# Attention steps in a fused attention and SwiGLU kernel: value products in a step of their own, PSUM banks dealt out anew

## The chip, the core and the metric

The kernel runs on one core of one Trainium2 chip. Its engines work side by side, each through its own queue in program order: TensorE (PE in the profile, its weight loads PEld), VectorE (DVE), ScalarE (ACT), GpSimd (POOL) and SyncE (SP), which here issues all DMAs. Matrix products are written to PSUM, which has eight banks of 128 partitions by 512 float32 values; DVE and ACT read them from there. The metric is the device time of one execution in microseconds (us). The kernel before took 1760.38 us, the median of three runs from 1759.78 to 1762.22.

## The reference, cut to what matters

The output is a gated mix of two branches of the same input x (2048 rows, 576 columns).

```
g = sigmoid(sum(x * gate_w))                 # one value a row
out = g * A(x) + (1 - g) * B(x)
B:  (silu(x @ w_gate) * (x @ w_up)) @ w_down          # inner width 4608
A:  32 heads of 18 columns, 4 segments of 512 rows; within a segment
    p = softmax(q @ k.T * scale + mask);  a_dot = p @ v
    a_mem = (phi(q) @ M) / (phi(q) @ z + 1e-6)        # memory of earlier segments
    o = sig(beta) * a_mem + (1 - sig(beta)) * a_dot;  then o @ wo
```

Computation is float32 in effect: operands are split into a high and a low part (`split`: ACT copies the high part, DVE subtracts it to get the low one), and three products are added.

## The kernel before, in words

There are three stages. The first (to about 212 us) makes q, k, v, the memory terms and stores them to DRAM. The second, the main loop, runs to about 1650 us and holds the change. The last mixes the branches and applies `wo`.

**The main loop** goes twice (two halves of the rows, 0 and 1) over 36 slices f of the inner width: 72 positions. A position makes seven products (`seven`, lines 973 to 981, seven matmuls of 512 columns each, numbered 0 to 6 here; a Strassen-like scheme for gate and up) in banks 0, 1 and 2. Between them ACT and DVE copy and combine the sums: line 1035 (ACT copies product 0 out of bank 0; product 2 then adds into that bank, so it has to wait for the copy), 1038, 1042, 1045, 1049, then two Silu calls at lines 1052 and 1054. Silu and Exp are in different tables of ACT, so line 1052 begins with a table load and `exp_table` (line 971) with another.

**Beats.** After each product but one `tick()` is called, eight times in a position (beats 0 to 7; beats 5 and 6 stand together after product 5). A beat first runs the small work that was deferred to it (`due`: weight splits, lines 231 to 252; hidden splits, lines 117, 118, 920, 921; stores), then down groups, then steps of attention.

**Down groups.** After every third slice the 16 down groups of these three slices come due (`feed`), and the next position, a down position, runs them: two in each of beats 2 and 3, three in each of beats 4 to 7 (`SHARE`). There are 11 such positions in each half; what is left runs at the halves' ends. A group is nine matmuls of 320 or 256 columns into one bank (line 837), then one DVE addition of that bank into `ya` (line 842). Groups take banks 3 and 4 in turn (`pair_tile`), so a group waits for the addition of the group two before it.

**Attention** is the generator `att_gen`, advanced step by step. A unit is two heads of a segment, 64 units in all. A unit has five score banks, numbered z; each is filled by one or two matmul calls (`s_bank`, line 713) and reduced by DVE to a bound a row (line 719). One step later ACT takes the exponential out of the bank into `pe` (`e_bank`, line 731) and POOL masks the diagonal (line 739); three steps after the scores (`PL`) DVE casts it to `p` and POOL subtracts for the low part (`p_bank`, lines 745, 746); five steps after (`XL`) SP issues a DMA transpose to `pt` (`x_bank`, line 750). Eight steps after the scores (`VL`), in the step of the last bank, `v_unit` multiplies the unit's five `pt` tiles with the values (40 short matmuls, lines 761, 762) and DVE reduces the sum (line 768). `o_step` scales, and a DMA stores the result.

So a unit takes five steps, and the score and value banks are taken in turn from 5, 6 and 7 (`ts_tile`), six takings a unit. There are three buffers of `pe`, four of `p`, eight of `pt`.

How fast the generator goes is set by `credit` in `beat`: each allowed slot adds a number from `TICK`, and a step runs when the sum reaches 1. Down positions have a slot after the first and the third group of a beat and one in beats 0 and 1; other positions have one in each of beats 0 to 4.

```
TICK = ((0.48, 0.85), (0.39, 0.85))      # (half 0, half 1), (no groups due, groups due)
```

When the generator ends, `c_open` loads what the last stage needs.

Of the kernel before, what the change touches and what calls it, by code (L numbers as in the profile page):

```python
# [12 lines left out]
F32 = mybir.dt.float32  # L13
F32R = mybir.dt.float32r
BF = mybir.dt.bfloat16
F16 = mybir.dt.float16
# [4 lines left out]
P = 128  # L21
# [4 lines left out]
L = 512  # L26
NSEG = 4
# [9 lines left out]
NB = 8 * NSEG  # L37
NST = 2
PL = 3
XL = 5  # L40
VL = 8
KEPT = 2
HALF = ((2, 3), (0, 1))
TICK = ((0.48, 0.85), (0.39, 0.85))
QUIET = (5, 6, 7)
LEAD = 3
HIGH = (2, 3, 3, 7, 7, 8, 9)
# [19 lines left out]
def gated_mix(ctx, tc, xT, xrest, wf, wfr, wfh, wd, wv, wo, beta, cmask, ident, bmask, out):  # L67
# [32 lines left out]
    def banks(*ids):  # L100
        turn = cycle(ids)
        return lambda shape=(P, L): ps.tile(list(shape), F32, name=f"bank{next(turn)}")
# [3 lines left out]
    pair_tile = banks(3, 4)  # L106
# [4 lines left out]
    a_tile = banks(0)  # L111
    x_tile = banks(1)
    y_tile = banks(2)
    ts_tile = banks(5, 6, 7)

    def split(hi, lo, src):
        nc.scalar.activation(hi, src, AF.Copy)
# [57 lines left out]
    VP, accs, cur, mbs = {}, {}, {}, []  # L175

    def stack_loads(u):
        s, b = divmod(u, 16)
        r = []
        for kind, t, terms in ((0, qst, (0, 0, 1)), (1, kst, (2, 1, 2))):  # L180
            d = stk[kind, s, 2 * b * DH:2 * b * DH + 2 * DH]
            r.append((t[u % NST][0:3 * DH], d.rearrange("(j r) z n -> (r z) j n", r=DH)))
            for n, z in enumerate(terms):
                r.append((t[u % NST][(3 + n) * DH:(4 + n) * DH], d[:, z].rearrange("(j r) n -> r j n", r=DH)))
        return r
# [7 lines left out]
    def v_fetch(k):  # L193
        VP[k] = ap.tile([P, 4, 8, 3, E], BF, name="v")
        nc.sync.dma_start(VP[k], vd[k // 4, k // 2 % 2][:, :, 8 * (k % 2):8 * (k % 2) + 8])
# [481 lines left out]
    with ExitStack() as st:  # L677
        cps = []
# [24 lines left out]
        ap = pool(ast, "ap", 2, side="right")  # L703
        SPLAN = [[(0, 0, 3)], [(0, 1, 3)], [(384, 0, 0), (0, 0, 2)], [(384, 1, 0), (0, 1, 2)], [(0, 0, 1), (256, 1, 1)]]

        def s_bank(z):
            u, n = divmod(z, 5)
            qs, ks = qst[u % NST], kst[u % NST]
            m = mbs[u % 2]
            t = ts_tile()  # L710
            for c, pr, i in SPLAN[n]:
                w = P * (i + 1)
                nc.tensor.matmul(t[:, c:c + w], qs[:KR, pr, P * i:P * i + P], ks[:KR, pr, 0:w],  # L713
                                 start=True, stop=True)
            for c, pr, i in SPLAN[n]:
                w = P * (i + 1)
                k = pr * 4 + i
                scr = kp.tile([P, L], BF, name="scr", bufs=1)
                nc.vector.tensor_tensor_reduce(scr[:, :w], t[:, c:c + w], cm[:, L - w:L], -SCALE, 3.0e38,  # L719
                                               OP.add, OP.min, m[:, k:k + 1])  # L720
            cur["t", z] = t

        def e_bank(z):
            u, n = divmod(z, 5)
            m = mbs[u % 2]
            t = cur.pop(("t", z))
            pe = ap.tile([P, L], F32, name="pe", bufs=3)
            for c, pr, i in SPLAN[n]:
                w = P * (i + 1)
                k = pr * 4 + i  # L730
                nc.scalar.activation(pe[:, c:c + w], t[:, c:c + w], AF.Exp, bias=m[:, k:k + 1], scale=SCALE)  # L731
            first, step = ((384, 0), (384, 0), (256, 128), (256, 128), (128, 256))[n]
            if step:
                d = bass.AP(tensor=pe.tensor, offset=pe.offset + first, ap=[pe.ap[0], [step, 2], [1, P]])
                pat = [[0, 2], [-1, P]]
            else:
                d = pe[:, first:first + P]
                pat = [[-1, P]]
            nc.gpsimd.affine_select(d, d, pattern=pat, compare_op=OP.is_ge, fill=0.0, base=0, channel_multiplier=1)  # L739
            cur["e", z] = pe  # L740

        def p_bank(z):
            pe = cur.pop(("e", z))
            p = cur["p", z] = ap.tile([P, 2, L], F16, name="p", bufs=4)
            nc.vector.tensor_copy(p[:, 0], pe)  # L745
            nc.gpsimd.tensor_sub(p[:, 1], pe, p[:, 0])  # L746

        def x_bank(z):
            pt = cur["x", z] = ap.tile([P, 8, P], F16, name="pt", bufs=8)
            nc.sync.dma_start_transpose(pt, cur.pop(("p", z)).rearrange("p a n -> p (a n)"))  # L750

        def v_unit(u):
            g, hf = divmod(u, 2)
            s, b = divmod(u, 16)
            t = ts_tile([P, 2, 4, 3 * E])
            todo = [(5 * u + n, pr, i, j, c // P + j) for n in range(5) for c, pr, i in SPLAN[n] for j in range(i + 1)]
            for n, (z, pr, i, j, c) in enumerate(todo):
                h = 2 * b + pr
                v = VP[4 * s + h // 8][:, j, h % 8].rearrange("p t e -> p (t e)")
                pt = cur["x", z]  # L760
                nc.tensor.matmul(t[:, pr, i, :], pt[:, c], v, start=(n == 0), stop=False, skip_group_check=True)  # L761
                nc.tensor.matmul(t[:, pr, i, 0:2 * E], pt[:, 4 + c], v[:, 0:2 * E], start=False,  # L762
                                 stop=(n == len(todo) - 1), skip_group_check=True)
            for n in range(5):
                cur.pop(("x", 5 * u + n))
            if hf == 0:
                accs[g] = ap.tile([P, 2, 8, E], F32, name="acc")
            nc.vector.tensor_reduce(accs[g][:, hf], t.rearrange("p a i (t e) -> p (a i) e t", t=3),
                                    axis=AX.X, op=OP.add)

        sends = []

        def o_step(g):
            s, b = divmod(g, 8)
            rz = ap.tile([P, 4, 4], F32, name="rz", bufs=1)
            av = accs.pop(g).rearrange("p r (a i) e -> p (r a) i e", i=4)
            nc.vector.reciprocal(rz, av[:, :, :, DH])
            nc.gpsimd.tensor_mul(rz, rz, omg[:, 4 * b:4 * b + 4])
            ob = ap.tile([P, 4, 4 * DH], F32, name="ob", bufs=1)
            ov = ob.rearrange("p i (h e) -> p h i e", e=DH)  # L780
            nc.gpsimd.tensor_mul(ov, av[:, :, :, 0:DH], rz[:, :, :, None].to_broadcast([P, 4, 4, DH]))
            d = atd[4 * s:4 * s + 4, :, 4 * b * DH:4 * (b + 1) * DH]
            sends.append((d.rearrange("i p n -> p i n"), ob))

        def att_gen():
            N = 10 * NB
            for tau in range(N + VL + 5):
                u, n = divmod(tau, 5)
                if tau % 10 == 4 and sends:
                    nc.sync.dma_start(*sends.pop(0))  # L790
                if n in (2, 3) and u + 1 < 2 * NB:
                    for d in stack_loads(u + 1)[4 * (n - 2):4 * n - 4]:
                        nc.sync.dma_start(*d)
                z = tau - VL
                if z % 20 == 0 and 0 <= z < N and z // 20 + 1 < 4 * NSEG:
                    v_fetch(z // 20 + 1)
                if 0 <= z - 3 and (z - 3) % 10 == 9:
                    o_step((z - 3) // 10)
                if 0 <= tau - PL < N:
                    p_bank(tau - PL)  # L800
                if 0 <= tau - 1 < N:
                    e_bank(tau - 1)
                if z % 5 == 4 and 0 <= z < N:
                    v_unit(z // 5)
                if tau < N:
                    s_bank(tau)
                if 0 <= tau - XL < N:
                    x_bank(tau - XL)
                yield
            for z in sends:  # L810
                nc.sync.dma_start(*z)
# [15 lines left out]
        def down_group(c, i, hf, hs, ws, ya, half):  # L827
            b, k = divmod(i, 4)
            cs = (slice(0, 320), slice(320, D))[hf]
            t = pair_tile([P, 320])[:, :cs.stop - cs.start]  # L830
            n = 0
            for f in range(CH * c, CH * c + CH):
                hh, hl = (z[:, b, P * k:P * k + P] for z in hs[half, f])
                d = ws[half, f]
                dh, dl = d[:, 0], d[:, 1]
                for p, q in ((hh, dh), (hh, dl), (hl, dh)):
                    nc.tensor.matmul(t, p, q[:, cs], start=(n == 0), stop=(n == 3 * CH - 1))  # L837
                    n += 1
            if c == 0:
                nc.vector.tensor_copy(ya[:, i, cs], t)  # L840
            else:
                nc.vector.tensor_add(ya[:, i, cs], t, ya[:, i, cs])  # L842
            if c == FT // CH - 1 and hf and half == 0:
                stores.append((ffd[i], ya[:, i]))
# [248 lines left out]
        for n in range(17):  # L1093
# [6 lines left out]
            if n:  # L1100
                tt = order[n - 1]
                ff = ffs.pop(n - 1)
                for hf in range(2):
                    c = slice(288 * hf, 288 * hf + 288)
                    t = chain_tile()
# [67 lines left out]
```

## Time and profile before

| what | value |
|---|---|
| median of three runs | 1760.38 us (1759.78 to 1762.22) |
| the profiled execution's own time | 1760.2 us |
| its span, first to last instruction | 1758.5 us |
| PE, PEld busy | 1720.8, 1482.1 us |
| DVE, ACT, POOL busy | 1362.9, 1096.9, 937.6 us |
| granted clock of TensorE, mean | 0.997 |

The profile is of one execution. Matmuls are pipelined and their ends are modelled: a 512-column matmul is drawn 0.39 us long while its successor starts 0.23 us after it. So PE's busy time hides short waits, and a wait shows on PE with about 0.16 us missing; the weight loads (PEld) show the same wait from their side.

### The profile page before, as it was taken

The numbers are of one execution on the slowest core, as the hardware profiler recorded it, in microseconds if no ns is written. First come the engines' busy times: TensorE is split into PE (matmuls) and PEld (weight loads), VectorE is DVE, ScalarE is ACT, GpSimd is POOL, SyncE is SP. The second block draws the span as 40 slices with busy tenths as digits, with TensorE's granted clock in tenths as the row PEclk, the third lists the DMA queues.
The fourth block names the chain that finished last, engine by engine and source line by source line (L and its number), as shares of the span: only waits on it lengthen the run. The fifth ranks groups of instructions, "written<-read, shape, count | busy, mean of one in ns | idle before, by whom it ended". The sixth has DMA issues, their size and how long they took to land.

```text
span 1758.5 us, 35163 instructions
## 1 busy us (share of the span) xinstructions
PE 1720.8 (98%) x11868; PEld 1482.1 (84%) x11868; DVE 1362.9 (78%) x3239; ACT 1096.9 (62%) x2201; POOL 937.6 (53%) x1194
## 2 busy tenths in 40 slices
PE   9999999999999999999998999999999999999999
PEld 7898978888878878878887888888888888888899
DVE  6666578888898888878888777887887778876655
ACT  7665575775676577567656657665765577566511
POOL 4434646666565666656556555555555555553221
PEclk9999999999999999999999999999999999999999
DMA  8653488998987888798779977776777778665544
GB/s 286 231 178 130 159 284 181 215 226 180 222 211 179 208 195 205 159 221 195 172 186 240 288 156 165 184 167 157 164 187 163 133 180 192 152 134 140 164 133 140
DMA packets 524005, 328.08 MB, mean 187 GB/s; under 512 B 411184, under 2 KB 460336, under 8 KB 523824
## 3 DMA queue, kind: packets, MB, share of 16 engines
q1 hardware_dynamic: 523824, 325.83, 74.3%
q8 instruction: 93, 1.52, 0.4%
q14 instruction: 88, 0.72, 0.1%
HBM read 165.76 MB, written 76.09 MB: 138 GB/s over the span
## 4 chain that ended last, share of the span: by engine, by line
PE 66%; ACT 11%; DVE 11%; issue 4%; DMA 3%; POOL 3%; SPq 1%; POOLq 0%; DVEq 0%; ACTq 0%
PE bank L978 23%; PE bank L837 22%; PE bank L140 9%; PE bank L981 4%; PE bank L713 3%; PE bank L761 2%; DVE hl L921 2%; ACT L971 2%; DVE scr L719 2%; ACT L1052 2%; DVE p L745 1%; PE bank L762 1%; ACT pe L731 1%; DMA pt<-p 1%; POOL p L746 1%
## 5 line engine op out<-in xcount | busy, mean ns | idle before, releaser
L746 POOL TENSOR_TENSOR p<-pe,p 128x512 f16<-128x512 f32 x320 | 377.4, 1179 | 479.2 <-DVE p L745 455.5
L837 PE MATMUL bank<-dw,hh 128*128 128x320 f32 (+1 forms) x2304 | 490.8, 306 | 15.2 <-DVE ya L842 8.4
L837 PEld LDWEIGHTS bank<-dw,hh 128*128 128x128 f32 x2304 | 378.2, 189 | 38.9 <-DVE ya L842 19.7
L731 ACT ACTIVATE pe<-bank,mb 128x512 f32<-128x512 f32 (+3 forms) x512 | 247.2, 523 | 249.1 <-POOL p L746 189.6
L837 PE MATMUL bank<-dw,hl 128*128 128x320 f32 (+1 forms) x1152 | 340.4, 296 | 0.3 <-DVE hl L118 0.3
L719 DVE CUSTOM_DVE_ANT_0 scr<-bank,cm 128x512 bf16<-128x512 f32 (+3 forms) x512 | 248.1, 485 | 7.5 <-PE bank L713 0.8
L842 DVE TENSOR_TENSOR ya<-bank,ya 128x320 f32<-128x320 f32 x352 | 158.1, 453 | 88.1 <-PE bank L837 87.3
L837 PEld LDWEIGHTS bank<-dw,hl 128*128 128x128 f32 x1152 | 217.8, 189 | 0.6 <-DVE hl L118 0.6
L981 PE MATMUL bank<-xr,rh 128*128 128x512 f32 x504 | 196.7, 390 | 0.0
L739 POOL TENSOR_SCALAR_AFFINE_SELECT pe<-pe 128x256 f32<-128x256 f32 (+1 forms) x320 | 147.8, 462 | 12.6 <-ACT pe L731 9.4
L745 DVE CAST p<-pe 128x512 f16<-128x512 f32 x320 | 142.7, 446 | 6.5 <-DMA pt<-p 6.5
L245 POOL TENSOR_TENSOR ws<-raw 128x256 f32<-128x256 f32 x140 | 120.3, 860 | 24.6 <-DVE wo__22862 L252 4.1
L713 PE MATMUL bank<-kst,qst 108*128 108x512 bf16 (+3 forms) x512 | 124.8, 305 | 0.0
L921 DVE TENSOR_TENSOR hl<-row,hh 128x512 fp32r<-128x512 f32 x120 | 111.1, 926 | 10.6 <-ACT hh L920 10.4
L981 PEld LDWEIGHTS bank<-xr,rh 128*128 128x128 f32 x504 | 94.9, 188 | 20.4
L1045 ACT ACTIVATE row<-bank 128x512 f32<-128x512 f32 x72 | 43.1, 599 | 87.9 <-PE bank L981 87.9
L1050 DVE TENSOR_TENSOR row<-bank,row 128x512 f32<-128x512 f32 x72 | 49.6, 689 | 58.5 <-ACT bank L1049 58.0
L1049 ACT ACTIVATE bank<-bank 128x512 f32<-128x512 f32 x72 | 41.9, 582 | 82.6 <-PE bank L981 82.2
L1052 ACT ACT_TABLE_LOAD x72 | 92.4, 1283 | 1.3
L971 ACT ACT_TABLE_LOAD x72 | 92.4, 1283 | 1.0
L140 PE MATMUL bank<-xo,qhi 128*128 128x512 f32 x264 | 83.1, 396 | 0.0
L355 POOL TENSOR_TENSOR q<-qr,q 128x512 bf16<-128x512 f32 x36 | 44.4, 1234 | 70.5 <-ACT q L354 61.4
(2165 smaller groups left out, 4130.4 us busy)
## 6 DMA issues: line engine op xcount, KB each, us to landing
raw<-in_wf_dram SPq DMA_DIRECT2D x140, 256.0 KB
rh<-rc SPq DMA_DIRECT2D x72, 336.0 KB
dc<-dw SPq DMA_DIRECT2D x36, 576.0 KB
dw<-dc SPq DMA_DIRECT2D x36, 576.0 KB
stk<-q SPq DMA_DIRECT2D x32, 384.0 KB
draw<-in_wd_dram SPq DMA_DIRECT2D x36, 288.0 KB
rc<-rt SPq DMA_DIRECT2D x42, 224.0 KB
vd<-vps SPq DMA_DIRECT2D x8, 912.0 KB
```

Source lines behind the costliest of these rows:

```text
L140: nc.tensor.matmul(t, st[n], mv[n], start=(n == 0), stop=(n == 13))
L713: nc.tensor.matmul(t[:, c:c + w], qs[:KR, pr, P * i:P * i + P], ks[:KR, pr, 0:w], start=True, stop=True)
L719: nc.vector.tensor_tensor_reduce(scr[:, :w], t[:, c:c + w], cm[:, L - w:L], -SCALE, 3.0e38, OP.add, OP.min, m[:, k:k + 1])
L731: nc.scalar.activation(pe[:, c:c + w], t[:, c:c + w], AF.Exp, bias=m[:, k:k + 1], scale=SCALE)
L739: nc.gpsimd.affine_select(d, d, pattern=pat, compare_op=OP.is_ge, fill=0.0, base=0, channel_multiplier=1)
L745: nc.vector.tensor_copy(p[:, 0], pe)
L746: nc.gpsimd.tensor_sub(p[:, 1], pe, p[:, 0])
L837: nc.tensor.matmul(t, p, q[:, cs], start=(n == 0), stop=(n == 3 * CH - 1))
L842: nc.vector.tensor_add(ya[:, i, cs], t, ya[:, i, cs])
L921: defer(k + 1, lambda: nc.vector.tensor_sub(lo, src, f32(hi)))
L978: nc.tensor.matmul(t, w[:, p, z], x[z][:, q], start=first and n == 0, stop=False, skip_group_check=True)
L981: nc.tensor.matmul(t, rem[:, RPOS[j]], XR[j], start=False, stop=True, skip_group_check=True)
```

## The change

- A unit takes six steps: five with a score bank (`at` gives its number, or none), and the sixth (n = 5) for `v_unit` alone, without scores. The lags in steps of `e_bank`, `p_bank` and `x_bank` stay 1, 3 and 5; steps without a bank are skipped over. `VL` goes; the value products of a unit come in the sixth step of the next unit, 7 steps after its last score bank, 2 after its last transpose was issued (8 and 3 before).
- `TICK` is raised by about a sixth, so that 384 and some steps fit where 320 and some were.
- Scores and values have banks 5 and 6; down groups have 3, 4 and 7 until the last stage opens.
- `pe` has four buffers (was three), `pt` seven (was eight).
- The stack loads go out three, three and two a step in steps 1 to 3 of a unit (four and four in steps 2 and 3 before); `v_fetch`, `o_step` and the stores move to other steps.

```diff
-VL = 8
-TICK = ((0.48, 0.85), (0.39, 0.85))
+TICK = ((0.57, 1.0), (0.47, 1.0))
...
-    ts_tile = banks(5, 6, 7)
+    ts_tile = banks(5, 6)
+    group_tile = banks(3, 4, 7)
...
-            pe = ap.tile([P, L], F32, name="pe", bufs=3)
+            pe = ap.tile([P, L], F32, name="pe", bufs=4)
...
-            pt = cur["x", z] = ap.tile([P, 8, P], F16, name="pt", bufs=8)
+            pt = cur["x", z] = ap.tile([P, 8, P], F16, name="pt", bufs=7)
...
         def att_gen():
-            N = 10 * NB
-            for tau in range(N + VL + 5):
-                u, n = divmod(tau, 5)
-                if tau % 10 == 4 and sends:
+            N = 12 * NB
+
+            def at(t):
+                return 5 * (t // 6) + t % 6 if 0 <= t < N and t % 6 < 5 else None
+
+            for tau in range(N + 10):
+                u, n = divmod(tau, 6)
+                if n == 2 and sends:
                     nc.sync.dma_start(*sends.pop(0))
-                if n in (2, 3) and u + 1 < 2 * NB:
-                    for d in stack_loads(u + 1)[4 * (n - 2):4 * n - 4]:
+                if 1 <= n <= 3 and u + 1 < 2 * NB:
+                    for d in stack_loads(u + 1)[3 * n - 3:3 * n]:
                         nc.sync.dma_start(*d)
-                z = tau - VL
-                if z % 20 == 0 and 0 <= z < N and z // 20 + 1 < 4 * NSEG:
-                    v_fetch(z // 20 + 1)
-                if 0 <= z - 3 and (z - 3) % 10 == 9:
-                    o_step((z - 3) // 10)
-                if 0 <= tau - PL < N:
-                    p_bank(tau - PL)
-                if 0 <= tau - 1 < N:
-                    e_bank(tau - 1)
-                if z % 5 == 4 and 0 <= z < N:
-                    v_unit(z // 5)
-                if tau < N:
-                    s_bank(tau)
-                if 0 <= tau - XL < N:
-                    x_bank(tau - XL)
+                if n == 2 and u > 1 and u % 2 == 1 and (u - 3) // 2 < NB:
+                    o_step((u - 3) // 2)
+                z = at(tau - PL)
+                if z is not None:
+                    p_bank(z)
+                z = at(tau - 1)
+                if z is not None:
+                    e_bank(z)
+                z = at(tau)
+                if z is not None:
+                    s_bank(z)
+                if n == 5 and 1 <= u <= 2 * NB:
+                    v_unit(u - 1)
+                    if u % 4 == 1 and u // 4 + 1 < 4 * NSEG:
+                        v_fetch(u // 4 + 1)
+                z = at(tau - XL)
+                if z is not None:
+                    x_bank(z)
                 yield
...
-            t = pair_tile([P, 320])[:, :cs.stop - cs.start]
+            t = (pair_tile if cps else group_tile)([P, 320])[:, :cs.stop - cs.start]
```

## The prediction

> **What bounds the kernel now.** I read the page's busy times first, then windows by stage, the list of waits, the chain, and the timeline round one down position in each half.
>
> ```profile
> PE 1720.8 (98%) x11868; PEld 1482.1 (84%) x11868; DVE 1362.9 (78%) x3239; ACT 1096.9 (62%) x2201; POOL 937.6 (53%) x1194
> ```
>
> TensorE is the bound, and the change gives it the same matmuls. All it can move is time in which PE waits. Windows, each from the first to the last down matmul of a position, and two stretches between (length, then busy time of PE, PEld, DVE, ACT, POOL):
>
> ```profile
> 581.90:612.10 30.20, 29.94 (x266) 27.45 (x265) 25.09 (x69) 13.97 (x29) 17.74 (x25) 1.00 0.85 190
> 612.10:643.40 31.30, 30.78 (x173) 23.62 (x172) 27.97 (x61) 27.04 (x55) 19.61 (x24) 1.00 0.84 206
> 519.30:550.70 31.40, 30.58 (x267) 27.59 (x265) 25.88 (x70) 14.11 (x29) 18.60 (x27) 1.00 0.85 196
> 766.20:798.90 32.70, 30.51 (x267) 27.54 (x265) 25.74 (x70) 14.20 (x29) 18.58 (x27) 1.00 0.85 175
> 1227.00:1256.70 29.70, 29.70 (x171) 23.75 (x171) 24.62 (x54) 24.52 (x50) 15.94 (x20) 1.00 0.72 195
> 1256.70:1286.50 29.80, 29.74 (x265) 27.36 (x263) 24.65 (x66) 13.93 (x28) 17.73 (x24) 1.00 0.73 125
> ```
>
> Three positions take 61.5 us in half 0 and 59.5 in half 1 with the same products: half 0 has some 2 us of waiting in each of its 11 rounds, half 1 little. Two windows of half 0 are longer still, by 1.2 and 2.5 us over the first row. DVE is busy 83% in down positions and 89% between, so it lags. The waits (total, times, longest): the first row of the whole run, then four of PE and PEld from 212 to 900 us, then three from 900 to 1650:
>
> ```profile
> ACT pe L731 <- POOL p L746: 189.6, 115, 4.7
> PE bank L978 <- ACT bank L1035: 6.6, 11, 0.8
> PE bank L837 <- DVE ya L842: 4.7, 12, 1.4
> PEld bank L978 <- ACT bank L1035: 12.6, 19, 1.2
> PEld bank L837 <- DVE ya L842: 11.1, 24, 1.7
> PE bank L837 <- DVE ya L842: 3.1, 7, 0.9
> PEld bank L837 <- DVE ya L842: 7.8, 18, 1.3
> PEld bank L978 <- ACT bank L1035: 0.5, 2, 0.3
> ```
>
> PE's row counts only what lies behind the modelled end, some 0.16 us late, and leaves short waits out; PEld's is the nearer one. Down groups wait for `ya` 18.9 us (11.1 + 7.8; at least 4.7 + 3.1 = 7.8). Products wait for ACT's copy in line 1035 between 6.6 and 13.1 us; I take the middle, 9.6. No row has a score or value matmul waiting for its bank.
>
> **The change, part by part.**
>
> *Third bank for down groups: -18.9.* A row of the chain gives two groups:
>
> ```profile
> 346.40 2.43 PE bank L837 x18
> ```
>
>  A group then waits for the addition three groups back. In beats 4 to 7 the third group comes 1.6 us after the first one's end (a group and a score), while the addition and a step's DVE work have to fit between; with three banks a group and a product more lie there, some 2.8 us (two groups take 2.43, a product 1.6). The worst wait listed is 1.7. So all of it goes. What is late next on DVE is the score's reduction, counted below. Its floor is -7.8.
>
> *Four `pe`: ACT loses its 189.6 us of waiting.* A `pe` is reused a step after its cast now, two or three steps (of some 2.8 us) after the change; the longest wait is 4.7. Worth nothing on ACT itself, but it brings line 1035's copy forward. Here is the start of a down position in half 0:
>
> ```profile
> 573.66 0.84 ACT L731 ACTIVATE pe<-bank,mb 128x256 f32<-128x256 f32 x2 [0.49 <-POOL p L746]
> 579.54 0.58 ACT L1035 ACTIVATE bank<-bank 128x512 f32<-128x512 f32 x1
> 580.88 0.67 ACT L731 ACTIVATE pe<-bank,mb 128x512 f32<-128x512 f32 x1
> 577.37 0.39 PE L713 MATMUL bank<-kst,qst 108*128 108x512 bf16 x1
> 578.99 0.39 PE L981 MATMUL bank<-xr,rh 128*128 128x512 f32 x1
> 580.17 1.65 PE L978 MATMUL bank<-xo,wo__7569 128*128 128x512 f32 x6 [0.80 <-ACT bank L1035]
> ```
>
> Product 0 ends at 577.37, product 1 at 579.22 (its last matmul's start and 0.23). From the exponential at 573.66 to the copy ACT never rests. So without the 0.49 us, and without the 0.84 where the new credits put no exponential into beat 4 before, the copy ends at 0.5 to 1.3 us earlier, and most of the wait at 580.17 goes: -9.6 of line 1035.
>
> *Two banks for scores: +25.* A score then needs the exponential of the score two steps back, which ACT gets only one step before. That is short where two steps are one product apart: beats 0 and 1 of a down position, where the credits now always put steps: a down position has 12 slots, which made 10 steps at 0.85 and make 12 at 1.0, one a slot; an ordinary one has five slots at 0.57 or 0.47, two or three steps. Half 1's start of a down position:
>
> ```profile
> 1432.11 0.39 PE L713 MATMUL bank<-kst,qst 108*128 108x512 bf16 x1
> 1432.65 0.58 ACT L1035 ACTIVATE bank<-bank 128x512 f32<-128x512 f32 x1
> 1433.72 0.39 PE L981 MATMUL bank<-xr,rh 128*128 128x512 f32 x1
> 1433.99 0.66 ACT L731 ACTIVATE pe<-bank,mb 128x512 f32<-128x512 f32 x1
> ```
>
> Product 0 ended at 1432.11, and beat 1's score could start at 1433.95; beat 0's exponential ends at 1434.65, or 0.18 later as two pieces (0.84). The wait is 0.7 to 0.9. Adding up the credits position by position, of half 1's 11 down positions two are safe (a score without exponential at beat 0), five pay 0.8, two 1.5 (ACT has an exponential in beat 4 before), one 0.85 and one 0.1 (value products, which last 1.05, at beat 0): 8.0. In half 0 the exponential ended at 581.55, 2.3 after product 1; less the 0.49 or 1.3 gained above it is 1.0 for three positions, 1.9 for one, 1.1 for two and 0.2 for one with values at beat 0: 7.3. Of its four safe positions two keep 0.9 of line 1035's wait together. All four pay at beat 2, where the bank waits for beat 0's reduction and an exponential behind it (the two PE rows give the 1.05 of the values too):
>
> ```profile
> 583.21 0.20 PE L761 MATMUL bank<-v,pt 128*128 128x57 bf16 x1
> 584.26 0.38 PE L713 MATMUL bank<-kst,qst 108*128 108x128 bf16 x2
> 582.62 0.68 DVE L719 CUSTOM_DVE_ANT_0 scr<-bank,cm 128x512 bf16<-128x512 f32 x1
> ```
>
> The reduction ended at 583.3, its exponential could end at 584.0, and the score came at 584.26, which without the 0.8 of line 1035 is 583.5. Less what ACT gains, the wait is 0.2 twice and 0.75 twice: 1.9. Five ordinary positions of half 0 have steps in neighbouring beats: two at 1.3 and three at 0.8, estimated from the same rows, 5.1. The sum is 8.0 + 7.3 + 0.9 + 1.9 + 5.1 = 23.2, and I add 1.8 for places that I haven't found: 25. Ends: half of it, if ACT runs ahead; 40, if ACT gains nothing (7 times 1.3 more, and the same at the five).
>
> Beat 5 is the next tightest place. The exponential of beat 4's last score comes behind both table loads:
>
> ```profile
> 596.05 0.84 ACT L731 ACTIVATE pe<-bank,mb 128x256 f32<-128x256 f32 x2 [2.54 <-POOL p L746]
> 597.53 0.39 PE L981 MATMUL bank<-xr,rh 128*128 128x512 f32 x1
> 600.73 1.25 ACT L731 ACTIVATE pe<-bank,mb 128x512 f32<-128x512 f32 x2
> ```
>
> The first of the two at 600.73 (0.67 long) ended 3.65 after product 5 (597.53 and 0.23); beat 5's second score comes 3.9 after it (three groups of 1.2 and a score). It is costed at nothing, covered by 0.25 us and by what the wait for `pe` at 596.05 took; if that cover is gone, each 0.2 us costs 4 over 22 positions.
>
> ```profile
> L1052 ACT ACT_TABLE_LOAD x72 | 92.4, 1283 | 1.3
> ```
>
> The page's row of these loads has 1283 ns each and 1.3 us of idle time before all 72. The Trainium skill (ScalarE: Activation LUTs, What ACT_TABLE_LOAD costs) adds a drain of 1.38 us to a load's 1.28; by that rule beat 5 would wait about 1 us in 22 positions, some 22 more, 1777, but the row shows no drain, and I give it no chance.
>
> *Transposes: -3 and +1.* DVE's cast needs a `p` whose transpose has landed. Three times in half 0 that transpose was issued late and the chain went through it (start, length):
>
> ```profile
> 283.77 4.57 DMA pt<-p
> 530.76 4.80 DMA pt<-p
> 777.70 6.10 DMA pt<-p
> ```
>
> The two later ones lie in the two long windows: 3.7 us together, and SP stood before the last at stack loads and the value fetch of the same step. The change spreads the loads over three steps, takes the fetch to a step without them, and in four cases of five gives a `p` three steps instead of two after its transpose's issue: -3. On the other side `v_unit` comes two steps after its last transpose (three before). In half 0 the transpose of beat 3 goes out late:
>
> ```profile
> 588.48 0.39 PE L713 MATMUL bank<-kst,qst 108*128 108x128 bf16 x2
> 590.35 2.20 SPq L793 DMA_DIRECT2D kst<-stk  x4
> 592.67 1.25 SPq L750 DMA_TRANSPOSE pt<-p  x1
> ```
>
> That is 4.2 us behind PE's score (588.48); with 4 us to land, `v_unit` in beat 4's second slot, 7.2 after, would wait about 1; two stack loads fewer (1.1) end that in most of the four cases. I take +1; it could be 10, if SP comes later.
>
> *The rest: +0.5.* DVE, POOL and SP get the same instructions. Seven `pt` suffice, since at most six are held when the next is asked for with the value step done. By the credits the generator ends one beat later, so the last stage's loads start up to 1.6 us later, beside products that are still running.
>
> Sum: -18.9 - 9.6 + 25 - 3 + 1 + 0.5 = -5. The profiled execution took 1760.2 us (span 1758.5), 0.2 under the median of 1760.38. So 1755.3.
>
> **The rivals.**
>
> 1. *Two score banks cost more than the third group bank brings.* ACT doesn't come forward, since its time to line 1035 is set by the table loads and splits; then half 0 pays 2.3 at its positions: 40 in place of 25, +15, and 1770. It decides once the new waits exceed 31 us, 1.4 a down position. For it: ACT ran without a pause from 573.66 on. Against: the pause was at that very place. The Trainium skill (Perfetto Trace Analysis, Optimization Strategy) reads the same gap, repeated, as too little PSUM for the next tile; the `ya` rows agree, and by that rule the gap may as well appear at the scores.
> 2. *The change doesn't do what it says:* the `ya` waits are DVE's lag (89% busy between), and PE, let go, waits for DVE at the next product. Then a third of 18.9 comes back, +6: 1761, no change that can be told.
> 3. *ACT, free of 115 waits, runs ahead* and the waits at beat 1 halve: -12, 1743. Against: in half 1 no `pe` wait lies ahead of the copy, and the 0.8 us stand.
> 4. *Value products wait for transposes* in most of half 0's 17 value steps in down positions, 0.6 us each: +10, 1765.
>
> **How the numbers follow.** Forecast 0.42, by itself 1750 to 1759; rival 1 0.24, rival 2 0.18, rival 3 0.11, rival 4 0.05. 0.2% of 1760.38 is 3.5 us, about what a measurement can tell. Faster: 0.36 of the forecast's and rival 3, 0.47. Same: 0.06 of the forecast's, 0.13 of rival 2 and 0.02 of rival 1: 0.21. Slower: 0.32. The range leaves out half of rival 3 and the upper third of rival 1: 1745 to 1770.
>
> **What would show it.** In the profile after: no waits for `ya` in line 837 before 1650 us; `pe` waiting for `p` down from 189.6 to under 40; new rows of score matmuls waiting for `pe`, longest about 2 us, at beat 1 of down positions, 15 to 30 us in all; line 1035's rows under 4; the 31.4 and 32.7 windows back to some 30.5. Waits at beat 5, or for `pt`, or at line 978 for DVE would make it wrong.

## The result and the profile after

The changed kernel takes 1763.57 us, the median of 22 runs (1761.71 to 1766.21), against 1761.54 for the kernel before, timed beside it. The ratio is 1.0014, with a 95% interval of 1.0008 to 1.0020: slower by 2 us, inside the 0.2% that I called no change. The forecast was 1755.3. One of the 22 runs of the kernel before took 4328.71 us; the record gives no reason, and the ratio leaves it out. The profiled execution of the changed kernel took 1765.94 us, 2.4 above its median (span 1764.2, mean granted clock 0.993); the one of before had a clock of 0.997.

In the changed kernel lines after 790 carry numbers 7 higher: 837 is 844, 842 is 849, 978 is 985, 1035 is 1042 (4 higher still, past the edit, in the kernels whose order in a beat is changed). TensorE's waits (total, times, longest), three of the rows from 212 to 900 us and two from 900 to 1650:

```profile
PE bank L713 <- ACT pe L731: 8.5, 12, 1.2
PE bank L761 <- ACT pe L731: 4.6, 5, 1.8
PE bank L985 <- ACT bank L1042: 0.7, 3, 0.2
...
PE bank L761 <- ACT pe L731: 6.3, 3, 4.1
PE bank L713 <- ACT pe L731: 4.8, 7, 1.1
```

No down group waits for `ya` any more. In its place scores and value products wait for a bank, which ACT's exponential into `pe` frees. Products wait little for a transposed `pt` (1.0 us in three waits from 212 to 900 us). On the page of the profile ACT's row for line 731 has another releaser now, and the table load is as it was:

```profile
L731 ACT ACTIVATE pe<-bank,mb 128x512 f32<-128x512 f32 (+3 forms) x512 | 246.1, 522 | 227.3 <-DVE mb L719 224.5
...
L1059 ACT ACT_TABLE_LOAD x72 | 92.4, 1283 | 1.3
```

The 189.6 us in which ACT waited for `p` are gone, but ACT isn't ahead: it now waits 224.5 us for DVE's bound. The windows that answer to those of before (three down positions, and the third row the stretch between two of them):

```profile
521.90:550.80 28.90, 28.71 (x226) 26.51 (x225) 24.69 (x68) 13.82 (x27) 18.49 (x27) 1.00 0.85 196
582.90:612.00 29.10, 28.77 (x226) 26.58 (x225) 24.81 (x68) 13.85 (x27) 18.42 (x27) 1.00 0.86 182
612.00:644.90 32.90, 31.25 (x211) 24.90 (x210) 26.69 (x60) 27.55 (x56) 16.60 (x21) 1.00 0.89 207
768.20:796.70 28.50, 28.50 (x225) 26.46 (x224) 24.73 (x65) 12.79 (x25) 18.34 (x27) 1.00 0.88 176
```

From first to last down matmul a position got 1.1 to 4.2 us shorter; the stretch between, which holds beats 0 and 1 of the next down position, got 1.6 longer (32.9 against 31.3).

To balance the loop I took the start of every matmul from the first product of position 3 to the last product of position 71: each pause beyond the usual distance between matmuls of that pair of lines is put to the instruction that released it, where the trace names one. The pauses without a name come to 55 us in both kernels (60 with six steps on the old banks), and the named ones, in us, are:

| TensorE waits for | forecast of the change | before | after | six steps, old banks | after, with the steps first |
|---|---|---|---|---|---|
| `ya` (down groups) | -18.9 | 18.0 | 0 | 25.9 | 0 |
| `pe` (banks of scores, values), in beats | +25 | 0 | 23.1 | 0 | 6.5 |
| `pe`, between the halves | none | 0 | 5.6 | 0 | 3.8 |
| hidden values, between the halves | none | 5.2 | 0 | 2.5 | 0 |
| the copy of line 1035 | -9.6 | 9.1 | 2.6 | 3.1 | 2.2 |
| transposes | -2 | 0 | 1.9 | 1.5 | 0.5 |
| others | 0 | 1.2 | 0.5 | 1.5 | 1.1 |
| this stretch of the loop in all | -5.5 | 1395.4 | 1396.1 | 1401.5 | 1376.4 |

The last two columns are kernels from the experiments. So some 30 us of named waits went and some 30 came (33.5 before, 33.7 after), and the loop came out even, 0.7 longer. Of the 5.7 us between the two profiled spans (1758.5 and 1764.2) another 2.3 lie ahead of this stretch and 2.8 behind it. There the changed kernel's run has one and two half-rate windows of the clock more (last section), each worth up to 1.7 us by my estimate; inside the stretch it has one more too, between the halves.

### The profile page after: what moved, and what is told of

Same layout as the page of the kernel before. It is cut to its first block, busy times and chain, and to the rows that moved or that the text cites. A ratio compares the mean times of both kernels' runs of the same rounds, so it can differ in the third digit from the quotient of the medians.

```text
span 1764.2 us, 34937 instructions
## 1 busy us (share of the span) xinstructions
PE 1720.6 (98%) x11868; PEld 1490.4 (84%) x11868; DVE 1366.7 (77%) x3239; ACT 1095.4 (62%) x2201; POOL 933.7 (53%) x1194
## 4 chain that ended last, share of the span: by engine, by line
PE 76%; ACT 11%; DVE 4%; DMA 3%; issue 3%; POOL 2%; SPq 1%; DVEq 0%; ACTq 0%; POOLq 0%
PE bank L985 27%; PE bank L844 25%; PE bank L140 10%; PE bank L988 4%; PE bank L713 3%; PE bank L761 2%; ACT L1059 2%; ACT pe L731 1%; ACT L978 1%; PE bank L762 1%; PE bank L399 1%; ACT row L1059 1%; DMA pt<-p 1%; ACT bank L1042 1%; PE bank L445 1%
## 5 line engine op out<-in xcount | busy, mean ns | idle before, releaser
L844 PEld LDWEIGHTS bank<-dw,hh 128*128 128x128 f32 x2304 | 384.4, 191 | 14.1 <-ACT hh L117 3.1
L731 ACT ACTIVATE pe<-bank,mb 128x512 f32<-128x512 f32 (+3 forms) x512 | 246.1, 522 | 227.3 <-DVE mb L719 224.5
L739 POOL TENSOR_SCALAR_AFFINE_SELECT pe<-pe 128x256 f32<-128x256 f32 (+1 forms) x320 | 150.2, 470 | 31.4 <-ACT pe L731 25.9
L713 PE MATMUL bank<-kst,qst 108*128 108x512 bf16 (+3 forms) x512 | 125.2, 306 | 13.3 <-ACT pe L731 13.2
L988 PEld LDWEIGHTS bank<-xr,rh 128*128 128x128 f32 x504 | 94.7, 188 | 20.5
L928 DVE TENSOR_TENSOR hl<-row,hh 128x512 fp32r<-128x512 f32 x120 | 100.9, 841 | 10.7 <-ACT hh L927 10.3
L761 PE MATMUL bank<-v,pt 128*128 128x57 bf16 x1280 | 77.6, 188 | 12.0 <-ACT pe L731 10.9
L713 PEld LDWEIGHTS <-qst 108*128 108x128 bf16 x512 | 35.8, 98 | 63.1 <-issue 47.0
```

The costliest lines, as they stand in the source:

```text
L988: nc.tensor.matmul(t, rem[:, RPOS[j]], XR[j], start=False, stop=True, skip_group_check=True)
```

## The experiments

All times are medians; the kernel before was timed beside each at 1761.1 to 1761.7, and ratios are against it. A difference of 2 us between two of my kernels can't be told, nor one of 3 us where both ran only four or five times.

**The parts of the change, one at a time.** Four `pe` and seven `pt` alone, on the kernel before:

```diff
-            pe = ap.tile([P, L], F32, name="pe", bufs=3)
+            pe = ap.tile([P, L], F32, name="pe", bufs=4)
-            pt = cur["x", z] = ap.tile([P, 8, P], F16, name="pt", bufs=8)
+            pt = cur["x", z] = ap.tile([P, 8, P], F16, name="pt", bufs=7)
```

> The kernel before with four tiles of exponentials and seven of turned p, nothing else of the change. Theory: ScalarE's waits for a tile pe fall from 189.6 us to under 40, the waits of TensorE for the hidden copy (line 1035) from 9.6 to under 4, the waits for ya stay at 16 to 19; the time falls by 4 to 6 us from 1761.5, to 1755.5 to 1757.5. Rival 'the copy waits move': what the copies no longer wait for pe they wait for scores, time within 1 us. Rival 'seven pt is one too few': value products wait longer for their turned p and the time rises by 2 us or more.

Measured: 1758.44 us, ratio 0.9979 (0.9970 to 0.9988), 3.2 us less. The mechanism held, the size didn't: by the starts of the matmuls the waits for the copy of line 1035 fell from 9.1 to 5.2, not under 4. Undoing it in the changed kernel (`bufs=3`, `bufs=8`):

> The changed kernel with three pe and eight pt, as before its change; banks and six steps stay. Theory: the fourth pe was worth 3.2 us alone and is worth more where two score banks are freed by exponentials: ScalarE waits for a pe 100 us or more again, TensorE's waits for score banks rise above 30 us, and the time is 3 to 12 us above the changed kernel's 1763.6. Rival 'without effect, the step for values gives the slack': within 1 us.

1764.80 us (1.0020, 1.0012 to 1.0029): 1.2 more than the changed kernel, which can't be told. ACT waits for `p` again, and next to nothing follows, nearest to the rival:

```profile
ACT pe L731 <- POOL p L746: 104.8, 55, 4.2
```

The new banks alone, on the kernel before with its five steps:

```diff
-    ts_tile = banks(5, 6, 7)
+    ts_tile = banks(5, 6)
+    group_tile = banks(3, 4, 7)
...
-            t = pair_tile([P, 320])[:, :cs.stop - cs.start]
+            t = (pair_tile if cps else group_tile)([P, 320])[:, :cs.stop - cs.start]
```

> The kernel before with the new banks alone: two for scores and value products, three for down groups; five steps a unit, so that one step in five still issues value products and scores together, and three pe. Theory 'two banks need a step of their own for values': where both stand in one step, the value products take the bank that the scores before last have not yet left; TensorE waits for pe 1 to 3 us at 20 or more of the 64 value steps, and the time rises by 40 to 100 us, to 1800 or above. Rival 'the exponentials are early enough': ya waits go (22 us) and score waits of about 25 come, 1758 to 1768.

1787.53 us (1.0153, 1.0139 to 1.0167), 26 more. Scores wait in both halves (its lines are one higher):

```profile
PE bank L714 <- ACT pe L732: 15.8, 21, 2.1
...
PE bank L714 <- ACT pe L732: 18.9, 23, 1.7
```

44 waits of 0.8 us on average. It is scores that wait, hardly the value products (1.2 us), and the price lies below the theory's range and above the rival's. Without the sixth step (and with three `pe`) the banks lose 26 us, with it (and four `pe`) they gain 7. The reverse, the changed kernel with its old banks:

```diff
-    ts_tile = banks(5, 6)
-    group_tile = banks(3, 4, 7)
+    ts_tile = banks(5, 6, 7)
+    group_tile = banks(3, 4)
```

> The changed kernel with the banks of the kernel before its change: three for scores and value products, two for down groups; six steps a unit, four pe and seven pt stay. Theory 'the banks trade one wait for another': the 24.6 us that TensorE waited for two score banks go, down to under 6, and the waits of down groups for ya come back at 16 to 19 us; the time falls by 5 to 9 us, to 1755 to 1759. Rival 'the third down bank is worth its whole 18.9' (score waits would be hidden slack): the time rises by 10 or more. Rival 'neither is on the path': within 1 us of 1763.6.

1770.73 us (1.0044, 1.0032 to 1.0057), 7.2 more than the changed kernel: my theory had the sign wrong, and the rival's 10 or more weren't reached. The weight loads' rows, for the two halves:

```profile
PEld bank L844 <- DVE ya L849: 19.3, 19, 1.9
...
PEld bank L844 <- DVE ya L849: 8.5, 9, 4.5
```

That is 27.8 where the kernel before had 18.9 and the one with four `pe` 18.6. So on two banks the six steps lengthen the waits for `ya`, and the third bank takes the longer wait away. Down positions have 12 steps in place of 10 there (`TICK` went up by 18 to 21%, a fifth rather than a sixth); that this is the reason isn't shown by itself. In a chain of single edits: four `pe` -3.2, six steps +12.3 (1758.44 to 1770.73), the banks -7.2, together +2.

**The order in a beat.** In beats 0 and 1 the attention's step is issued ahead of the deferred work. No down group stands in these beats.

```diff
+            first = k in (0, 1)
+            fns = due.popleft() if due else ()
-            for fn in due.popleft() if due else ():
+            for fn in () if first else fns:
                 fn()
...
+            for fn in fns if first else ():
+                fn()
```

> The changed kernel, but in the first two beats of each period the attention's step is issued ahead of that beat's hidden work instead of behind it. Theory 'two banks wait for late exponentials': the exponentials of the first steps stand ahead of ScalarE's hidden copies, the score waits at the positions of beats 1 and 2 fall from 15 to 20 us over the run to under 8, and the time falls by 5 to 10 us. Rival 'the wait only changes its place': the copies come later by as much, TensorE waits for the hidden values at line 1042 instead, 10 us or more, time within 2 us or up.

1745.13 us (0.9904, 0.9889 to 0.9920): 18.4 below the changed kernel, twice what I expected. The named waits for `pe` fall from 28.7 to 10.3 (table); what is left from 212 to 900 us, and from 900 to 1650, where 3.6 is the one between the halves:

```profile
PE bank L761 <- ACT pe L731: 2.3, 5, 1.0
PE bank L713 <- ACT pe L731: 0.7, 2, 0.3
...
PE bank L761 <- ACT pe L731: 4.0, 2, 3.6
```

The timeline of one wait shows how. First the changed kernel at position 29 (start, length, engine, line), then the same place with the step first:

```profile
812.34 0.57 ACT L1042 ACTIVATE bank<-bank 128x512 f32<-128x512 f32 x1
812.86 0.40 ACT L249 ACTIVATE wo__11088<-ws 128x256 fp32r<-128x256 f32 x1
813.16 0.61 ACT L927 ACTIVATE hh<-row 128x512 fp32r<-128x512 f32 x1
813.68 0.66 ACT L731 ACTIVATE pe<-bank,mb 128x512 f32<-128x512 f32 x1
814.39 0.38 PE L713 MATMUL bank<-kst,qst 108*128 108x128 bf16 x2 [1.17 <-ACT pe L731]
```

```profile
800.72 0.58 ACT L1046 ACTIVATE bank<-bank 128x512 f32<-128x512 f32 x1
801.23 0.66 ACT L731 ACTIVATE pe<-bank,mb 128x512 f32<-128x512 f32 x1
801.80 0.40 ACT L249 ACTIVATE wo__11103<-ws 128x256 fp32r<-128x256 f32 x1
802.11 0.62 ACT L927 ACTIVATE hh<-row 128x512 fp32r<-128x512 f32 x1
801.94 0.38 PE L713 MATMUL bank<-kst,qst 108*128 108x128 bf16 x2 [0.34 <-ACT pe L731]
```

ACT doesn't pause in either. The exponential stood behind a weight copy and a hidden split; ahead of them it comes 0.83 us sooner after the copy of line 1042, and the wait falls from 1.17 to 0.34. The place is typical: of the 24 waits for `pe` of 0.4 us and more in the changed kernel (27 us), 22 end with an exponential ahead of which ACT had no gap, and in 21 of these a hidden split stands right ahead of it; in the other two ACT waited 1.06 us for DVE's bound. The later splits cost TensorE little: no other row of the table grows by more than 0.6 us. The edit moves the step's work on DVE and POOL ahead as well; no run takes that apart. Which beat it is, two runs tell (`k == 0`, then `k == 1`):

> The changed kernel with the attention's step ahead of the deferred hidden work in beat 0 alone. Theory 'the exponentials of beat 0 stand behind one weight sum's copy and one hidden split on ScalarE': they come 0.8 us earlier at every position with a step in beat 0, and that is most of the 18.4 us of the edit in both beats: 8 to 16 us less than 1763.6. Rival 'beat 1 carries it': within 4 us of 1763.6.

1746.23 us (0.9917, 0.9904 to 0.9931), 17.3 below the changed kernel, 1.3 more than the theory gave it at most.

> The same with beat 1 alone. Theory of beat 0: 2 to 8 us less than 1763.6, the two single edits together 14 to 22. Rival 'beat 1 carries it': 12 us or more less.

1759.99 us (0.9995, 0.9987 to 1.0004), 3.6 below, as the theory had it. Beat 0 carries nearly all. Is it a matter of the two banks? The same edit with the old banks on six steps:

> The six-step kernel with the banks of before (three for scores and values, two for down groups) and the attention's step ahead in the first two beats. Theory 'the order cures score waits and nothing else': there are none here, the waits for ya stay at 20 to 28 us and the time near 1770.7 (1768 to 1773). Rival 'the layout in six steps costs because its exponentials are late, whatever the banks': ya waits fall under 15 and the time comes to 1752 to 1758.

1753.45 us (0.9950, 0.9936 to 0.9963): 17.3 below 1770.73. My theory fell; the rival's size was right. With three score banks the late step reached TensorE by way of `ya`, whose rows fall from 27.8 to 13.3:

```profile
PEld bank L844 <- DVE ya L849: 10.5, 15, 1.3
...
PEld bank L844 <- DVE ya L849: 2.8, 7, 0.8
```

So order and banks act side by side: -17 to -18 with either banks, and -7.2 or -8.3 for the banks with either order. On five steps:

> The kernel before with the issue order alone: the attention's step ahead of the hidden work in the first two beats. Theory 'the order pays only where two score banks wait for exponentials': TensorE has no wait for pe here, the waits for ya stay at 15 to 20 us and those for the copy at line 1035 rise above 9.6; the time stays within 3 us of 1761.6. Rival 'the order pays by itself' (earlier exponentials shorten ScalarE's queue whatever the banks): 10 us or more less, 1752 or below.

1758.16 us (0.9979, 0.9971 to 0.9988), 3.4 less, just past the theory's bound, and not by its rows: the weight loads' waits for `ya` fell from 18.9 to 12.1, and those for the copy of line 1035 fell from 13.1 to 9.0 instead of rising. And with four `pe` as well:

> The kernel before (five steps, its banks) with four pe and seven pt and the attention's step ahead in the first two beats: the fourth corner to 1758.4 (four pe), 1758.2 (order) and 1753.5 (six steps and order on the same banks). Theory 'the six steps cost only through the late steps': both gains add here, 1754 to 1756.5, and the six steps are worth within 3 us of nothing once the order is mended. Rival 'the six steps gain by themselves': 1757 or above.

1759.15 us (0.9988, 0.9979 to 0.9997), in the rival's range. The two gains of 3 us don't add, and the order is worth little on five steps. In the first of the two kernels, from 212 to 900 us, the weight splits moved back make down groups wait:

```profile
PEld bank L837 <- DVE ya L842: 9.0, 22, 2.5
PEld bank L837 <- DVE dw L921: 5.8, 11, 0.8
```

With the order mended on both sides the six steps gain 5.7 us (1759.15 to 1753.45) instead of losing 12.3. Why they are so much more sensitive to it I can't show: by the credits 43 steps fell into beat 0 and 29 into beat 1 before, 49 and 44 after.

**Is it VectorE?** In the changed kernel DVE stood still behind a hidden split, with the attention's bound queued behind it, from 212 to 900 us:

```profile
DVE hl L118 <- ACT hh L117: 16.4, 11, 1.8
```

```diff
-            if q == CH - 1:
-                defer(2, lambda t=(hh[:, 0], hl[:, 0], sg0): split(*t))
-            else:
-                split_by(2, hh[:, 0], hl[:, 0], sg0)
+            split_by(2, hh[:, 0], hl[:, 0], sg0)
```

> The changed kernel with its own issue order, but every third position's first hidden split (line 117 and 118, issued together in beat 0 behind the third position of a group) is taken apart: VectorE's part of it follows one beat later, as at the other positions. Theory 'VectorE stands still behind the split': its wait for ScalarE's hh (16.4 us in 11 waits in the first half) falls under 6, the mask additions that stood behind it run up to 1.8 us earlier, the score waits of TensorE fall from 24.6 us by 8 or more and the time by 6 to 14 us from 1763.6. Rival 'it is ScalarE's order, the exponentials behind the hidden copies': the wait on VectorE goes, the exponentials do not come earlier by more than 0.5 us, time within 2 us of 1763.6.

1761.29 us (0.9997, 0.9988 to 1.0006), 2.3 below the changed kernel. The row is gone and the waits for `pe` hardly fell (`L713` from 8.5 to 7.2). That is nearest to the rival, ACT's order. The same edit on top of the fastest kernel, and the step first in every beat without down groups (`first = k in (0, 1) or not groups`), both with the later copies told of below:

> The fastest kernel so far (six steps, two score banks and three for down groups, attention's step ahead in the first two beats, two copies of wo later, 1741.8) with the hidden split taken apart as well. Theory 'the two edits mend the same wait': VectorE's wait for hh, 5.7 us here, goes, but little hangs on it; 0 to 3 us less. Rival 'they add': 6 us or more less.

> The same fastest kernel with the attention's step ahead of the hidden work in every beat that has no down group, not in the first two alone. Theory 'only the steps behind the hidden split were late': within 2 us of 1741.8. Rival 'every step gains by it': 5 us or more less; second rival 'hidden copies now come late': TensorE waits for the copy at line 1046 over 8 us and the time rises.

1751.51 us (0.9940, 0.9926 to 0.9954) and 1754.60 (0.9963, 0.9951 to 0.9976): 9.7 and 12.8 more. For the first neither theory nor rival had a rise; for the second only the second rival had it. In the one the low part comes too late for the first down group; in the other hidden copies come late, by less than the 8 us that the rival said:

```profile
PE bank L844 <- DVE hl L928: 4.7, 9, 0.7
```

```profile
PE bank L989 <- ACT bank L1046: 2.6, 5, 0.8
```

These rows explain half of the first loss and a fifth of the second; the rest stays open.

**The end of the loop.** In the profile after, the chain at the end runs through a load and a copy of `wo` ahead of the last hidden split:

```profile
1663.20 7.07 DMA raw<-in_wo_dram
1670.29 0.60 ACT wo L877
```

```diff
-            for tau in range(N + 10):
+            for tau in range(N + 9):
```

> The changed kernel, except that the attention's generator is left one empty step earlier (range(N + 9) for range(N + 10)), so that the last stage's loads and copies of wo are issued one beat sooner, as in the kernel before. Theory 'the end' (the handover to the last stage is what the prediction priced too low): from the last product of the loop to the end of the span 97.5 us goes back to 94.7 or so, TensorE's gap ahead of the last stage from 8.0 to about 4.4, no half-clock window at 1670, time 3 to 5 us below the changed kernel's 1763.6, so 1758.5 to 1760.5. Rival 'the prediction's +0.5' (the later loads cost up to 1.6 us): 0.5 to 1.6 less, so 1762 to 1763. Rival 'clock windows fall by chance': no change within 1 us, and the sum of half-clock time in the profile differs between runs without a pattern.

1765.19 us (1.0015, 1.0007 to 1.0024): nothing won. The wait went elsewhere: the earlier loads of `wo` now stand ahead of the last `rh` load in SP's queue, which is issued at 1652.55 us in place of 1644.08:

```profile
PE bank L988 <- DMA rh<-rc: 2.2, 1, 2.2
PE bank L844 <- ACT hh L117: 1.4, 1, 1.4
```

Then the two last copies of `wo` four beats later, with the step first and without it:

```diff
-            defer(n + 5, lambda: nc.scalar.activation(wos[hf][:, 0, :, c], box[0], AF.Copy))
-            defer(n + 7, lambda: nc.vector.tensor_sub(wos[hf][:, 1, :, c], box[0], f32(wos[hf][:, 0, :, c])))
+            defer(n + (5 if n < 8 else 9), lambda: nc.scalar.activation(wos[hf][:, 0, :, c], box[0], AF.Copy))
+            defer(n + (7 if n < 8 else 11), lambda: nc.vector.tensor_sub(wos[hf][:, 1, :, c], box[0], f32(wos[hf][:, 0, :, c])))
```

> The changed kernel with the attention's step ahead in the first two beats, and the last two copies of wo four beats later, so that ScalarE's last hidden split does not stand behind copies whose loads are still under way. Theory 'the handover waits for those copies': TensorE's gaps ahead of the last stage fall from 3.3 us (2.1 and 1.1) to under 1.5, ScalarE's split of hh starts right after its exponential table's load, and the time is 1 to 3 us below the 1745.1 of the same kernel with the copies where they were. Rival 'the last stage's products need those copies': the wait comes back at its first product with wo, time within 1 us.

> The changed kernel with its last two copies of wo four beats later and nothing else. Theory 'the end waits for those copies': ScalarE's last hidden split comes 1.5 us or more earlier, TensorE's gap ahead of the last stage falls from 2.9 us to under 1.5, and the time is 2 to 4 us below 1763.6, as it was 3.3 below 1745.1 with the other order. Rival 'the gap is filled by the clock and by the copies' later users': within 1 us.

1741.79 us (0.9889, 0.9876 to 0.9903) and 1763.05 (1.0009, 1.0000 to 1.0018). The first is 3.3 below its pair, the second 0.5. In the second the 2.9 us for which TensorE waited for the last hidden split in the changed kernel have become two waits of the same sum:

```profile
PE bank L844 <- DVE ya L849: 1.7, 1, 1.7
PE bank L844 <- ACT hh L117: 1.2, 1, 1.2
```

So the end isn't where the forecast was lost. In the kernel with the step first, whose profile has no half-rate window there, the stretch from the last product to the end took 95.5 us, against 94.7 before: 0.8, near the forecast's 0.5. Whether the later copies bring 3 us beside the new order stays open, as the two intervals overlap. The kernel with both is the fastest, 1.1% below the kernel before.

## Why the prediction was right or wrong

The forecast lay 8 us too low, and its sign was wrong. The mechanisms were mostly right; the step that failed is the term for the transposes, and the term for line 1035 was too large. By its own steps:

- *Third bank for down groups, -18.9:* held. `ya` waits went to nothing (18.0 by the starts of the matmuls). What I didn't see is that the six steps with two banks would have had 25.9.
- *Two banks for scores, +25:* held in size and place: 23.1 in the beats. By the starts of the matmuls 15.4 of it stand in beat 1 of down positions (forecast 8.0 + 7.3), 2.0 in beat 2 (1.9) and 5.8 in ordinary positions (5.1). But I took ACT's order as given. ACT was "without a pause", and that was the clue: an engine that never rests can still do the urgent thing first, and 17 of these 23 us went with the order. The Trainium skill (Perfetto Trace Analysis, Optimization Strategy) says that a repeated gap can mean too little PSUM for the next tile. The gap did move to the scores here, as the prediction allowed, and an order took 17 us of it away without a bank.
- *Four `pe`, line 1035, -9.6:* the wait was there (9.1), and 2.6 of it stayed; alone, four `pe` took 3.9 of it. I let the wait go as a whole on the evidence of one position. Why the rest stayed no run shows. (The middle of 6.6 and 13.1 is 9.9, not 9.6, and the five ordinary positions above come to 5.0, not 5.1; neither matters.)
- *Transposes, -3 and +1:* **the step that failed.** The two long windows were real, and they did shorten, but nearly all the time in them was already counted as waits for `ya`. The kernel before, in the windows 519.3 to 550.7 and 766.2 to 798.9:

```profile
PEld bank L837 <- DVE ya L842: 1.7, 4, 0.8
...
PEld bank L837 <- DVE ya L842: 3.2, 4, 1.7
```

 An ordinary window (581.9 to 612.1) has 0.8 in this row, so 0.9 and 2.4 of the 1.2 and 2.5 us by which the two are longer were waits for `ya`. TensorE is the bound, so a late transpose costs only through one of TensorE's waits, and those were in the sum: the -3 was counted twice. The +1 came as 1.9. This term, -2, measured +1.9; it was off by 3.9 us, more than any other priced term.
- *Between the halves:* not priced. Hidden values cost 5.2 us there before, and a value product that waits 4.1 for its bank, with a score, took their place (5.6). It came out even by chance. Before, then after:

```profile
PE bank L837 <- ACT hh L117: 2.5, 1, 2.5
PE bank L978 <- DVE bank L1042: 1.1, 1, 1.1
PE bank L837 <- DVE dw L921: 1.0, 1, 1.0
```

```profile
PE bank L761 <- ACT pe L731: 4.1, 1, 4.1
PE bank L713 <- ACT pe L731: 1.1, 1, 1.1
```

- *Beat 5 at nothing, table loads without a drain:* held; no wait for `pe` there, and the loads' row is unchanged.
- *The rest, +0.5:* I suspected it first, since the chain after shows 7 us of a load there. Moving the end and moving the copies brought nothing that can be told, and by the step-first profile it is 0.8.
- The misses in the loop are +3.9 (transposes), +3.1 (line 1035), +0.9 (`ya`) and +0.4 (between the halves), against -1.9 (scores in beats) and -0.7 (others): 5.7 of the 6.2 us between -5.5 and +0.7. Another 1.2 is the base: 1760.38 of three runs against 1761.54 of 22. That leaves 0.9 of the 8.3. The changed kernel's 22 runs had a mean clock of 0.9946, the kernel before 0.9956 to 0.9959 beside the experiments: some one half-rate window more a run, by my estimate at most 1.7 us.
- *The other rivals:* rival 1 (new waits over 31) didn't come. Rival 2's 1761 is nearer to the result than the forecast, but not by its mechanism, since the weight loads of the products wait less for DVE (line 1042, now 1049: 5.2 before, 1.2 after). Rival 3's halved waits didn't come, and of rival 4's 10 us 1.9 did.
- *What would show it:* `ya` gone, `pe` no longer waiting for `p`, scores waiting at most about 2 us within the beats, line 1035 under 4 (2.6 by the starts, 4.1 by the weight loads' rows) and the long windows below 30.5 were all seen. Of the signs against it waits for `pt` were seen, small (1.9). Nearly all signs held and the sum did not: signs tell that a mechanism is there, not that its terms are separate.

## What to carry to other kernels

Where one engine is the bound, price a change only through that engine's waits, each microsecond once; a late transfer or a slow helper is not a second term. When a buffer is taken away and the engine that frees it is busy, look at what stands ahead of the freeing instruction in its queue before counting the wait as the buffer's price: here 0.8 us of work that could wait, in one beat, was worth more than the whole deal of banks. Test the parts alone: six steps, banks and order were worth +12, -7 and -17 us, and the change as it was made showed 2.

## What the hardware showed

Windows in which TensorE's clock ran at half rate differ from run to run and blur small results: the 22 runs of the changed kernel had mean clocks from 0.992 to 0.996. The profiled one had seven such windows of 3.4 us ahead of its end (four of them in two pairs), the one of before three. Two profiles at the end of the loop, first the changed kernel, then the one with three `pe`; the column after the engines' busy times is the clock:

```profile
1666.80:1670.60 3.80, 1.78 (x13) 1.42 (x11) 2.70 (x4) 3.25 (x6) 2.01 (x2) 1.00 1.11 346
1670.60:1677.40 6.80, 5.87 (x22) 5.35 (x23) 3.75 (x8) 1.98 (x5) 3.30 (x4) 0.50 0.53 196
```

```profile
1670.90:1674.30 3.40, 3.22 (x12) 2.93 (x13) 3.04 (x7) 0.50 (x2) 1.66 (x2) 0.51 0.93 345
1674.30:1677.70 3.40, 3.40 (x27) 3.40 (x27) 0.92 (x2) 0.60 (x2) 1.68 (x2) 0.99 0.00 1
```

With one half-rate window instead of two the stretch from the last product to the end took 95.5 us instead of 97.4; without any it was 94.7 in the kernel before. That is the 2 to 3 us that made the end look guilty. The Trainium skill (TensorE: Matmul & The Clock Gate, What's actually happening) has windows of 3413 ns that run freely and gives half rate after an idle one. The length agrees: the half-rate stretches of these traces are 3.41, 6.83 and once 10.24 us long, but for the last, at the kernel's end. But the window ahead needn't be idle. On the 3.41 us grid of the 18 traces, all 72 windows with TensorE busy for less than 1.5 us (by the modelled ends) were followed by half rate, 8 of 10 from 1.5 to 1.7, 5 of 20 from 1.7 to 1.9, and 6 of 159 from 1.9 to 2.6. The changed kernel's window from 1667.2 to 1670.6 us, with 1.39 us busy, is one of the 72. By my estimate from these counts a pause of 2 us in a kernel that is bound by TensorE can cost up to half of 3.4 us more if it falls into one window, and nothing if two share it; no run tests this by itself.
